# Loading each token's channels once instead of twice, with a new assignment of channels to partitions

## The chip, the cores and the metric

One core of a Trainium2 chip. The metric is the device time of one execution, in microseconds (us). Kernels that are compared ran on the same chip in the same group; each group has its own runs of the kernel before. The profile's span starts and ends inside the execution. In most executions it is 1.7 to 1.9 us shorter than the device time, in a few 2.2 to 2.4 us.

TensorE multiplies matrices, and its results go to banks of a memory called PSUM; VectorE, ScalarE and GpSimd compute element by element. The DMA engines move data: a transfer is issued from the queue of an engine, is cut into pieces, each a contiguous run of bytes, and lands later. Memory on the core has 128 partitions (rows).

## The reference

A causal convolution along the sequence (7 taps, softmax-normalised, one set of taps for each group of 24 channels), then a two-layer network with an exact GELU between its matrices.

```python
x = randn(8, 4096, 192) * 0.1        # batch, sequence, channels
weight = randn(8, 7) * 0.3           # heads, taps
w = softmax(weight, axis=-1)
conv[b, s, h, g] = sum_k w[h, k] * x_padded[b, s + k, h, g]   # 24 channels g a head
h = conv.reshape(32768, 192) @ w_in  # 192 x 2048
out = gelu_exact(h) @ w_out          # 2048 x 192, out is float32
```

## The kernel before

Tokens run in two halves. A block takes w tokens of each half (w is 256 for blocks 0 to 5, then 512, 35 blocks in all). The 128 partitions are four quadrants of 32: quadrant q holds half q//2 of the tokens, and one of two sets of channels, by q%2. Each of the three slices p of a block has 64 channels a token half: partition j of the half, slice p, is channel 64p+j. So quadrant q%2=0 needs channels 0-31, 64-95 and 128-159, and q%2=1 the others. The load doesn't pick them out: each quadrant loads the whole rows (less 32 floats) in one contiguous run per partition, and x comes in twice.

```python
def load(e, n, qs=(0, 2, 1, 3), sm=None):      # e: the engine that issues
    mb = WS[n] // 32
    if n >= NX:
        e.wait_ge(S_TR, NP * (n - NX + 1))
    for q in qs:
        off = ((q // 2) * HALF + OFF[n]) * D + 32 * (q % 2)
        e.dma_start(
            ap(xin[n % NX], 32 * q * (TB // 32 * D),
               [[TB // 32 * D, 32], [1, mb * D - 32]]),
            ap(xt, off, [[mb * D, 32], [1, mb * D - 32]]),
        ).then_inc(sm or S_XIN[n % NX], 16)
...
# VectorE, slice p of block n: 32x32 transposes, tokens by channels -> channels by tokens
v.transpose(
    ap(xT[n % 2], p * XW + HL, [[NP * XW, 128], [1, w]]),
    ap(xin[n % NX], 64 * p, [[TB // 32 * D, 128], [D, w // 32], [1, 32]]),
).then_inc(S_TR)
```

Around it: VectorE convolves on the transposed x (in blocks 0 and 1 TensorE does that, with diagonal matrices), TensorE multiplies by W_in, ScalarE applies GELU, TensorE multiplies by W_out, and VectorE transposes the result for the store. Engines work in order. The start on GpSimd, whose queue also carries the transfers that convert to bf16, is

```python
for i in range(3):
    win_in(FP[i], FP[i + 1], S_WIN[i])     # W_in, 6 transfers
g.wait_ge(S_IDN, 2)
halo(0)                                    # needs block 0's transposes
load(g, 1, SW[1], S_XG[1])                 # 2 transfers
load(g, 2, SW[2], S_XG[2])                 # 4 transfers
g.dma_start(... wout ... woutt ...).then_inc(S_WOUT, 16)
halo(1)
load(g, 3, SW[3], S_XG[3])                 # 4 transfers
```

## Time and profile before

| | before |
|---|---|
| median of 3 runs | 687.19 us (686.70 to 687.27) |
| profiled execution | 687.63 us, span 685.8 us |
| TensorE busy | 677.9 us (99%) |
| VectorE busy | 563.0 us (82%) |

The rows of the page that the change touches, first the input transposes (after the bar: busy time, mean ns of one), then the transfers of x and W_out (KB each, median us from issue to landing):

```profile
L476 DVE STREAM_TRANSPOSE xT<-xin 128x512 f32<-128x512 f32 (+1 forms) x105 | 61.4, 635 | 2.4 <-issue 2.0
...
xin<-in_x_dram SPq DMA_DIRECT2D x116, 380.0 KB, 6.8
...
xin<-in_x_dram POOLq DMA_DIRECT2D x10, 188.0 KB, 5.9
wout<-in_moe_w_out_dram POOLq DMA_DIRECT2D x1, 768.0 KB, 11.2
```

A reader should see that the 116 large x loads alone are 45 MB for an x of 25.2 MB, and that they land in 6.8 us (median) while a block of 512 takes 20.7 us.

### The profile page before, as it was taken

To read this page: it belongs to the slowest core of one execution; us is meant where nothing else is said; L and a number is where in the kernel's file an instruction comes from. 1 tells how busy PE (TensorE), PEld (TensorE's weight loads), DVE (VectorE), ACT (ScalarE), POOL (GpSimd) and SP (SyncE) were. 2 spreads that over 40 slices of the span, in tenths; PEclk is the share of its full clock that TensorE was granted. 3 is DMA by queue.
4 is the path that set the end of the run, shared out by engine and by line. 5 is a ranking of instruction groups with operands and counts; after the bars stand their busy time and mean duration, and the time that the engine had idled before them with its cause. 6 is when DMAs were issued, how large, how long until landed. Compare 5 with 4: busy or idle time off the path is not lost.

```text
span 685.8 us, 27314 instructions
## 1 busy us (share of the span) xinstructions
PE 677.9 (99%) x12548; PEld 409.1 (60%) x12548; DVE 563.0 (82%) x914; ACT 532.0 (78%) x536; POOL 45.3 (7%) x97
## 2 busy tenths in 40 slices
PE   8999999999999999999999999999999999999997
PEld 4799755555555555555555555555555555555556
DVE  6999978888898888898888898888898888988602
ACT  6788987777787877778777877777878777777771
POOL 7110000000000000000000000000000000000000
PEclk9999999999999999999999999999999999999999
DMA  9657851456543566434566434565344665431224
GB/s 200 131 142 168 201 125 24 118 139 140 114 91 91 125 139 140 105 86 98 132 139 139 96 87 99 138 140 134 90 89 108 139 140 123 93 86 27 48 49 94
DMA packets 74418, 78.25 MB, mean 114 GB/s; under 512 B 64576, under 2 KB 69824, under 8 KB 70592
## 3 DMA queue, kind: packets, MB, share of 16 engines
q1 hardware_dynamic: 69776, 72.24, 46.0%
q0 software_dynamic: 3792, 3.50, 2.9%
q8 instruction: 98, 1.61, 1.1%
q10 hardware_dynamic: 736, 0.78, 0.4%
q14 instruction: 16, 0.13, 0.1%
HBM read 52.90 MB, written 25.17 MB: 114 GB/s over the span
## 4 chain that ended last, share of the span: by engine, by line
PE 94%; DMA 2%; ACT 1%; POOL 1%; issue 0%; DVE 0%
PE hp L681 47%; PE ob L745 42%; PE ob L712 5%; DMA wout<-in_moe_w_out_dram 2%; ACT gT L610 1%; DMA xin<-in_x_dram 1%; POOL xin L256 0%; POOL xTb L366 0%; ACT osb L225 0%; ACT L556 0%; DVE osb L245 0%; DVE osb L227 0%; DVE xT L476 0%
## 5 line engine op out<-in xcount | busy, mean ns | idle before, releaser
L610 ACT ACTIVATE gT<-hp 128x1024 bf16<-128x1024 f32 x512 | 522.9, 1023 | 135.2 <-PE hp L681 132.0
L681 PE MATMUL hp<-xc,win 64*64 64x512 bf16 (+2 forms) x6048 | 418.5, 366 | 1.0 <-ACT gT L610 0.7
L745 PE MATMUL ob<-gT,wout 64*64 64x512 bf16 x5376 | 366.3, 376 | 0.0
L506 DVE SCALAR_TENSOR_TENSOR acc<-xT,wcol,acc 128x512 f32<-128x512 f32 (+1 forms) x495 | 314.1, 699 | 0.0
L681 PEld LDWEIGHTS hp<-xc,win 64*64 64x64 bf16 (+1 forms) x6048 | 187.7, 106 | 135.6 <-ACT gT L610 2.1
L745 PEld LDWEIGHTS ob<-gT,wout 64*64 64x64 bf16 x5376 | 172.1, 118 | 123.0
L245 DVE STREAM_TRANSPOSE osb<-ob 128x512 f32<-128x512 f32 x84 | 74.0, 883 | 104.4 <-PE ob L745 104.4
L506 DVE SCALAR_TENSOR_TENSOR xc<-xT,wcol,acc 128x512 bf16<-128x512 f32 (+1 forms) x99 | 65.1, 712 | 0.0
L476 DVE STREAM_TRANSPOSE xT<-xin 128x512 f32<-128x512 f32 (+1 forms) x105 | 61.4, 635 | 2.4 <-issue 2.0
L372 POOL COPY xT<-xT 128x558 f32<-128x558 f32 x33 | 21.5, 652 | 579.6 <-DVE xT L476 579.6
L499 DVE TENSOR_SCALAR acc<-xT,wcol 128x512 f32<-128x512 f32 (+1 forms) x99 | 56.2, 619 | 1.1
L712 PE MATMUL ob<-wout,gT 64*128 64x192 bf16 x1024 | 52.2, 243 | 1.7 <-DMA wout<-in_moe_w_out_dram 1.4
L712 PEld LDWEIGHTS ob<-wout,gT 64*128 64x128 bf16 x1024 | 43.6, 94 | 7.9 <-DMA wout<-in_moe_w_out_dram 1.7
L355 POOL COPY xT<-xT 128x18 f32<-128x18 f32 x30 | 11.6, 386 | 1.1 <-DVE xc L459 1.1
L227 DVE COPY osb<-ob 128x384 f32<-128x384 f32 x4 | 2.2, 558 | 7.8 <-PE ob L712 7.8
L623 PE MATMUL hp<-warm 128*128 128x512 bf16 x16 | 6.3, 577 | 1.3 <-DVE warm L392 1.3
L225 ACT ACTIVATE osb<-ob 128x384 f32<-128x384 f32 x12 | 5.8, 486 | 0.0
L638 PE MATMUL ob<-xTb,dg 64*64 64x256 bf16 x84 | 5.3, 271 | 0.5 <-DVE xTb L452 0.5
L638 PEld LDWEIGHTS ob<-xTb,dg 64*64 64x64 bf16 x84 | 4.3, 107 | 1.6 <-DVE xTb L452 0.8
L623 PEld LDWEIGHTS hp<-warm 128*128 128x128 bf16 x16 | 2.1, 136 | 5.0 <-issue 3.6
L256 POOL DMA_DIRECT2D xin<-in_x_dram x10 | 5.0, 509 | 0.0
L437 DVE COPY win<-win 64x768 bf16<-64x768 bf16 (+1 forms) x6 | 3.2, 526 | 0.9 <-DMA win<-in_moe_w_in_dram 0.8
(32 smaller groups left out, 21.5 us busy)
## 6 DMA issues: line engine op xcount, KB each, us to landing
xin<-in_x_dram SPq DMA_DIRECT2D x116, 380.0 KB, 6.8
out_dram<-osb SPq DMA_DIRECT2D x112, 192.0 KB, 3.6
out_dram<-osb SPq DMA_DIRECT2D x56, 48.0 KB, 2.6
xin<-in_x_dram SPq DMA_DIRECT2D x12, 188.0 KB, 3.6
xin<-in_x_dram POOLq DMA_DIRECT2D x10, 188.0 KB, 5.9
wout<-in_moe_w_out_dram POOLq DMA_DIRECT2D x1, 768.0 KB, 11.2
win<-in_moe_w_in_dram POOLq DMA_DIRECT2D x4, 96.0 KB, 4.2
win<-in_moe_w_in_dram POOLq DMA_DIRECT2D x2, 192.0 KB, 5.2
```

The costliest lines, as they stand in the source:

```text
L245: v.transpose(ap(osb[m % 2], j, [[8 * C, 128], [C // 2, TB // 32], [NP, 32]]), bank(ring(m, j)),).then_inc(S_EV)
L355: g.tensor_copy(dst, ap(xT[(n - 1) % 2], WS[n - 1] + 31, [[NP * XW, 128], [XW, NP], [32, HB]],),).then_inc(S_HALO)
L372: g.tensor_copy(ap(t, 1, [[NP * tw, 128], [tw, NP], [32, HB], [1, 31]]), ap(t, WS[n], [[NP * tw, 128], [tw, NP], [32, HB], [1, 31]]),).the ...
L476: v.transpose(ap(xT[n % 2], p * XW + HL, [[NP * XW, 128], [1, w]]), ap(xin[n % NX], 64 * p, [[TB // 32 * D, 128], [D, w // 32], [1, 32]],) ...
L499: ins = v.tensor_scalar(a, src, wk, None, ALU.mult)
L506: ins = v.scalar_tensor_tensor(dst, src, wk, a, op0=ALU.mult, op1=ALU.add)
L610: a.activation(out=ap(gT[n % 2], i * c * 2 * w, dst), in_=ap(hp[u % 2], 0, src), func=AF.Gelu,).then_inc(S_GELU)
L623: t.matmul(hp[1][:, 0:512], warm[:, 0:128], warm[:, :])
L638: ins = t.matmul(bank(CONVB[n][p], r, w), dg[r, d0 : d0 + 64], xTb[PC[n]][r, x0 : x0 + w], start=(k == KS - 1), stop=(k == 0), tile_positi ...
L681: ins = t.matmul(hp[u % 2][fo : fo + fw, o : o + w], win[r, f1 : f1 + fw], xc[n % 2][r, p * TB : p * TB + w], start=(p == 0), stop=(p == N ...
L712: ins = t.matmul(bank(bb[sub], w=C), gT[m % 2][r, c0 : c0 + 128], wout[r, CH[i] * C : (CH[i] + 1) * C], start=(ph == 0 and i == 0), stop=( ...
L745: ins = t.matmul(bank(ring(m, j), slice(64 * h, 64 * h + 64), w), ap(wout, 64 * hf * NF * C + CH[i] * C + j, [[NF * C, 64], [NP, 64]],), g ...
```

## The change

Its intent is to load x once. A quadrant loads a contiguous half of a token's channels, and channel 3c+p of it becomes slice p of partition c. A load's run is then 96 floats a token (384 B), the transposes read every third float, and the rows of W_in and the channels of the taps follow.

```diff
+    DQ = D // 2
-        xin = [sbt("xin%d" % i, [128, TB // 32 * D], F32) for i in range(NX)]
+        xin = [sbt("xin%d" % i, [128, TB // 32 * DQ], F32) for i in range(NX)]
# load
-                off = ((q // 2) * HALF + OFF[n]) * D + 32 * (q % 2)
+                off = ((q // 2) * HALF + OFF[n]) * D + DQ * (q % 2)
-                        32 * q * (TB // 32 * D),
-                        [[TB // 32 * D, 32], [1, mb * D - 32]],
+                        32 * q * (TB // 32 * DQ),
+                        [[TB // 32 * DQ, 32], [DQ, mb], [1, DQ]],
-                    ap(xt, off, [[mb * D, 32], [1, mb * D - 32]]),
+                    ap(xt, off, [[mb * D, 32], [D, mb], [1, DQ]]),
# W_in
-                        ap(wint, hf * FH + c0, [[F, 64], [64 * F, NP], [1, c1 - c0]]),
+                        ap(wint, hf * FH + c0, [[NP * F, 64], [F, NP], [1, c1 - c0]]),
# taps
-                    ap(wch, 32 * (q % 2), [[D, 32], [64, NP], [1, 32]]),
+                    ap(wch, DQ * (q % 2), [[D, 32], [1, NP], [NP, 32]]),
# input transposes
-                        64 * p,
-                        [[TB // 32 * D, 128], [D, w // 32], [1, 32]],
+                        p,
+                        [[TB // 32 * DQ, 128], [DQ, w // 32], [NP, 32]],
```

## The prediction

> **What bounds the kernel now.** I read the page's busy row first, then the chain of work that ended last, then the waits, then the order of instructions on VectorE and GpSimd in the first 100 us.
>
> ```profile
> span 685.8 us, 27314 instructions
> PE 677.9 (99%) x12548; PEld 409.1 (60%) x12548; DVE 563.0 (82%) x914; ACT 532.0 (78%) x536; POOL 45.3 (7%) x97
> ...
> DMA packets 74418, 78.25 MB, mean 114 GB/s; under 512 B 64576, under 2 KB 69824, under 8 KB 70592
> ...
> PE 94%; DMA 2%; ACT 1%; POOL 1%; issue 0%; DVE 0%
> ```
>
> TensorE is busy for all but 8 us, and 94% of the chain is its own matmuls. So a transfer that is halved can win only where TensorE stands still. The table by stretch tells where that is (columns: stretch, length, busy time of PE, PEld, DVE, ACT, POOL, clock, DMA share, GB/s).
>
> ```profile
> 20.00:25.00 5.00, 3.61 (x76) 3.10 (x72) 5.00 (x14) 2.96 (x3) 0.27 (x1) 1.00 0.52 121
> 25.00:74.00 49.00, 48.87 (x1040) 45.81 (x1036) 48.82 (x107) 40.38 (x46) 4.11 (x9) 1.00 0.65 154
> ...
> 91.00:655.00 564.00, 564.00 (x10458) 320.18 (x10460) 474.21 (x723) 446.09 (x437) 24.93 (x51) 1.00 0.48 109
> ```
>
> From 91 to 655 us TensorE has no gap at all; from 20 to 25 us it is idle for 1.4 us. VectorE is full from 25 to 74 us, which will matter below. The chain names what the gap waits for:
>
> ```profile
> 8.22 3.01 POOL xin L256 x6
> 11.23 11.22 DMA wout<-in_moe_w_out_dram
> 22.50 0.67 PE ob L712 x12
> ```
>
> The first output matmul needs W_out. GpSimd issues that transfer at 11.23, behind six x loads, and it lands 11.22 us later because the DMA engines are saturated (share 1.0 and more in each 2 us stretch from 4 to 22 us). The waits give the share of this that TensorE feels: 1.4 us once, and no other wait of TensorE above 0.7 us.
>
> ```profile
> PE ob L712 <- DMA wout<-in_moe_w_out_dram: 1.4, 1, 1.4
> DVE osb L245 <- PE ob L745: 104.4, 30, 11.8
> ```
>
> The second line is VectorE's slack: in the steady state it stands about 3 us in each 20.7 us block for TensorE.
>
> **What the Trainium skill says.** Three places bear on it.
> "DMA: Bandwidth & Descriptors", Specifications, puts the smallest transfer at line rate at 512 B. The new pieces of x are 96 floats = 384 B. The trace has pieces of that size already, the output stores: from 620 to 640 us only one block's stores run, with a DMA share of 0.19, so 0.19 x 20 us x 16 engines / 2048 packets = 30 ns of an engine for one packet, or 786 KB in 3.8 us = 207 GB/s. The loads' 12160 B rows: the steady share 0.48 x 20.7 us = 9.9 us a block, less 3.8 for the stores, leaves 6.1 us for 1.556 MB = 255 GB/s. So small pieces are slower per byte, as the page has it, but only by a fifth, for half the bytes.
> "Advanced Engine Details and Errata", SBUF Cachelines, says lines are 16 bytes and that an access pattern which changes the line at each access pays. A step of three floats is 12 bytes: of four reads only two share a line. No transpose in the trace reads with that step, but the output transpose writes with it: 883 ns against 681 for the input transpose at the same 512 columns.
> "VectorE: DVE Perf Modes", the section on the TRN2 errata, gives PSUM sources 120 cycles of fixed cost against 58, so up to 65 ns of those 202 can be PSUM; the rest, 137 to 202 ns, is the step, if reading costs what writing costs. I take 0.17 us at 512 columns and 0.085 at 256 as my estimate.
>
> **The change, part by part.**
> *Loads of x.* A 512-token block goes from 4 x 32 rows of 12160 B to 4 x 512 pieces of 384 B: 1.556 MB and about 6.1 us of DMA time become 786 KB and, at 30 ns a piece, 3.8 us. A 256-token block goes from 770 KB (about 3.0 us at the same 255 GB/s) to 1024 pieces, 1.9 us. In all, x read falls from 49.8 MB to 25.2 MB, while the packets rise by 480 for each of 116 large issues and 224 for each of 24 small ones, 61,056 in all, to about 135,500. After 26 us nothing waits for these transfers: they are issued three blocks ahead (over 40 us) and land in under 9. Gain there: 0.
> *The start.* Blocks 0 to 3 are loaded before W_out lands. Four times 1.1 us less DMA time puts its landing at about 22.4 - 4.4 = 18.0, plus what its issue is delayed. TensorE arrives at 21.1. So the whole 1.39 us of the wait goes: -1.4 us.
> *GpSimd's descriptors.* Its ten x loads go from 32 pieces to 256. Two other issues give the price: 192 pieces took 655 ns (W_in), 2048 took 1394 (W_out): 0.40 ns a piece. So 490 ns becomes about 580, six of them before W_out are +0.54 us, still far from the 3 us it would need to bring the wait back.
> *Block 1.* VectorE stands 1.96 us before the transposes of block 1 (12.11 to 14.07); GpSimd's halo copy that they need ended at 12.89, so the load came last, and it comes sooner now. The halo copy moves to about 12.89 + 0.54 + 0.3 (next point) = 13.7. So block 1 starts some 0.3 us sooner; TensorE, which waited 0.51 us for it at 15.45, gains about 0.2: -0.2 us.
> *Taps and the first transposes.* The four 96-column transposes of the taps read with the step: 4 x 0.03 = +0.13 us; the three of block 0: 3 x 0.085 = +0.26. The first was started at 6.37, 0.04 us after VectorE had finished its previous work, so an earlier load of block 0 wins nothing, and the added time moves the first convolution by some 0.3 us. Most of it is met again in the waits between ScalarE and TensorE in block 0; the 0.2 above has it counted in.
> *W_in.* Same pieces, same bytes, another row order: 0.
> *Transposes, steady state.* 87 x 0.17 + 18 x 0.085 = +16 us of VectorE, busy 563 to about 579. Per block 0.5 us, out of its wait of 3 us before the first output transpose of a block. That wait is for TensorE's second pass, so what comes after it, the last convolution taps, keeps its distance to TensorE: 0 us.
> *Transposes, 25 to 91 us.* Here VectorE has no waits and its work runs a little ahead. Its results for block 6 were ready at 71.64 and TensorE took them up at 74.93: margin 3.3. Block 7: 87.15 and 90.97, margin 3.8. TensorE now arrives 1.6 us sooner; VectorE starts block 2 about 0.3 sooner, then carries 3 x 0.085 for each of blocks 3, 4, 5 and 3 x 0.17 for 6 and 7: +1.0 net by block 6, +1.5 by block 7. Left: 0.7 us in both. No loss, but nearly none to spare.
> *Store and load issue on the sync queue.* The loads' issue grows from 0.43 us to what a store of as many pieces takes, 0.8; the queue waits for 414 us of the span: 0.
> Sum: -1.4 - 0.2 = -1.6 us, so 687.19 - 1.6 = 685.6.
>
> **The rivals.**
> *The step costs VectorE more.* If each strided read took two cycles, 512 columns would cost 681 + 533 = 1214 ns. By block 7 VectorE would be 0.8 x 4 + 1.6 x 2 - 0.5 = 5.9 us later against a margin of 3.8: TensorE would wait some 2 us more than before in all, and the gain at the start is swallowed by the same wait. In the steady state 1.6 us a block still fits into 3. Time: about 689.5. For it: the page on cachelines, and a full VectorE from 20 to 74 us. Against it: the write with the same step costs 0.2 us, not 0.53.
> *GpSimd's descriptors cost more.* At 1 us an issue instead of 0.58, the halo copy of block 1 comes at 16 and TensorE loses about 2 us there; W_out, then issued at 14.3, still lands before TensorE comes. Time: about 687.5. For it: ten issues with eight times the pieces, and VectorE's copies of W_in run beside them. Against: 2048 pieces in 1.39 us.
> *Nothing at all moves*, because the first 20 us are set by VectorE and ScalarE and W_out's landing is bound by something other than bytes (its own 2048 pieces of 768 B): 687.2. Against: the DMA share of over 1.0 at 182 to 277 GB/s with four queued x loads in it.
> *VectorE becomes the bound* all along: it would need over 1 us more per transpose. 700 us or more; nothing in the profile speaks for it.
>
> **Range and chances.** Predicted 685.6. Best case, a free step and more won in block 0 and 1: 684.3. Worst within eight in ten, the step at two cycles: 689.5. A change of 2% is 13.7 us; TensorE's idle time is 8 us in all, of which the change touches 2, so faster by over 2% cannot follow (1%). Slower needs VectorE to become the bound (2%). Within 2%: 97%.
>
> **What would show it.** HBM read falls from 52.9 to about 28.3 MB and packets rise to about 135,500; if not, I read the loads wrongly. The wait of TensorE for W_out is gone and the transfer lands near 19 us. The input transpose of 512 columns takes 0.82 to 0.88 us and VectorE's busy time is near 579; over 1.1 us brings a wait of TensorE for the convolution near 73 or 89 us and makes the prediction wrong upwards. The x issues on GpSimd take near 0.58 us. VectorE's wait for TensorE before output transposes falls from 104 to about 90 us.

## More of the kernel before

The sync queue and ScalarE's queue each issue two of block 0's four loads.

## The result, and the profile after

| | before, same chip | changed | ratio (95% interval) |
|---|---|---|---|
| first measurement | 686.95 us, 4 runs | 686.56 us, 4 runs | 0.9998 (0.9981 to 1.0015) |
| control, run later | 686.51 us, 11 runs | 686.52 us, 5 runs | 0.9997 (0.9986 to 1.0009) |

A ratio is the mean time of one kernel's fast runs over that of the other's fast runs of the same rounds, so it isn't quite the ratio of the medians in the table. Within 0.2% the change does nothing to the time.

Its page, in the lines that answer to those of before:

```profile
span 684.5 us, 27314 instructions
## 1 busy us (share of the span) xinstructions
PE 677.3 (99%) x12548; PEld 409.0 (60%) x12548; DVE 580.5 (85%) x914; ACT 532.6 (78%) x536; POOL 46.0 (7%) x97
...
DMA packets 133234, 53.66 MB, mean 78 GB/s; under 512 B 127552, under 2 KB 132960, under 8 KB 133120
...
HBM read 28.31 MB, written 25.17 MB: 78 GB/s over the span
...
L478 DVE STREAM_TRANSPOSE xT<-xin 128x512 f32<-128x512 f32 (+1 forms) x105 | 78.5, 799 | 0.2 <-DMA xin<-in_x_dram 0.2
...
xin<-in_x_dram SPq DMA_DIRECT2D x116, 192.0 KB, 4.4
...
xin<-in_x_dram POOLq DMA_DIRECT2D x10, 96.0 KB, 2.7
wout<-in_moe_w_out_dram POOLq DMA_DIRECT2D x1, 768.0 KB, 8.6
```

The bytes read fell from 52.9 to 28.3 MB, loads land in 4.4 us instead of 6.8, and VectorE carries 17.5 us more. TensorE's work is the same.

By stretch (columns as in the prediction):

```profile
20.00:25.00 5.00, 4.92 (x100) 4.14 (x96) 5.00 (x14) 3.99 (x4) 0.27 (x1) 1.00 0.34 84
25.00:74.00 49.00, 48.93 (x1040) 45.88 (x1038) 48.86 (x105) 40.47 (x46) 3.62 (x8) 1.00 0.46 99
...
91.00:655.00 564.00, 564.00 (x10460) 320.21 (x10456) 490.34 (x727) 446.19 (x436) 25.97 (x53) 1.00 0.35 75
```

The start, in single lines: first of the kernel before, then of the changed one (start, length, engine, line; in square brackets: idle time before, and what ended it):

```profile
14.07 1.10 DVE L476 STREAM_TRANSPOSE xT<-xin 128x256 f32<-128x256 f32 x3 [1.96 <-issue]
```
```profile
12.49 1.20 POOL L383 DMA_DIRECT2D wout<-in_moe_w_out_dram  x1
12.59 1.34 DVE L478 STREAM_TRANSPOSE xT<-xin 128x256 f32<-128x256 f32 x3
21.11 0.67 PE L714 MATMUL ob<-wout,gT 64*128 64x192 bf16 x12
```

Block 1's transposes no longer wait, W_out is issued later than before (11.23), and the first output matmul has no wait.

In this profile the gap of 1.4 us between 20 and 25 us is gone. If that were the change's doing, it should be 1.3 us faster, as the two spans are (685.8 and 684.5). The timed runs don't show it. That contradiction is what the experiments had to settle.

The chain of waits of the changed kernel no longer goes through GpSimd and W_out, but through block 0's load and the first convolution:

```profile
2.04 4.96 DMA xin<-in_x_dram
7.00 0.02 issue
7.03 0.53 DVE xT L478
7.55 0.02 issue
7.58 0.43 ACT xTb L572
8.00 0.04 issue
8.04 2.50 PE ob L640 x42
```

Block 0, with half the bytes, lands at 7.00 us. Before, it landed at 6.34 (the chain there has a DMA piece from 1.70 of 4.64 us). The first convolution starts at 8.04 instead of 7.48.

### The profile page after: what moved, and what is told of

It is laid out like the page before. It is cut to its first block, busy times and chain, and to the rows that moved or that the text cites. A ratio compares the mean times of both kernels' runs of the same rounds, so it can differ in the third digit from the quotient of the medians.

```text
span 684.5 us, 27314 instructions
## 1 busy us (share of the span) xinstructions
PE 677.3 (99%) x12548; PEld 409.0 (60%) x12548; DVE 580.5 (85%) x914; ACT 532.6 (78%) x536; POOL 46.0 (7%) x97
## 2 busy tenths in 40 slices
DMA packets 133234, 53.66 MB, mean 78 GB/s; under 512 B 127552, under 2 KB 132960, under 8 KB 133120
## 3 DMA queue, kind: packets, MB, share of 16 engines
q0 software_dynamic: 3792, 2.56, 2.4%
## 4 chain that ended last, share of the span: by engine, by line
PE 96%; ACT 2%; DMA 1%; issue 0%; DVE 0%; SPq 0%
PE hp L683 47%; PE ob L747 42%; PE ob L714 6%; ACT gT L612 2%; PE ob L640 1%; DMA xin<-in_x_dram 1%; ACT osb L227 0%; DVE osb L247 0%; SPq L258 0%; DVE osb L229 0%; DVE xT L478 0%; ACT xTb L572 0%; SPq L795 0%; ACT xc L579 0%
## 5 line engine op out<-in xcount | busy, mean ns | idle before, releaser
L247 DVE STREAM_TRANSPOSE osb<-ob 128x512 f32<-128x512 f32 x84 | 73.7, 880 | 86.8 <-PE ob L747 86.8
L478 DVE STREAM_TRANSPOSE xT<-xin 128x512 f32<-128x512 f32 (+1 forms) x105 | 78.5, 799 | 0.2 <-DMA xin<-in_x_dram 0.2
L357 POOL COPY xT<-xT 128x18 f32<-128x18 f32 x30 | 11.6, 387 | 1.4 <-DVE xc L461 1.4
L324 POOL DMA_DIRECT2D win<-in_moe_w_in_dram x6 | 3.9, 651 | 0.0
```

Source lines behind the costliest of these rows:

```text
L247: v.transpose(ap(osb[m % 2], j, [[8 * C, 128], [C // 2, TB // 32], [NP, 32]]), bank(ring(m, j)),).then_inc(S_EV)
L357: g.tensor_copy(dst, ap(xT[(n - 1) % 2], WS[n - 1] + 31, [[NP * XW, 128], [XW, NP], [32, HB]],),).then_inc(S_HALO)
L478: v.transpose(ap(xT[n % 2], p * XW + HL, [[NP * XW, 128], [1, w]]), ap(xin[n % NX], p, [[TB // 32 * DQ, 128], [DQ, w // 32], [NP, 32]],),) ...
```

## The experiments

Four theories stood against each other. (A) The prediction's: halved bytes end the wait for W_out, worth 1.4 us. (B) The wait belongs to the one profiled execution and neither kernel. (C) Pieces, not bytes, decide how fast loads are. (D) The slower transposes cost time.

### The changed kernel again, as control

No edit.

> The changed kernel once more, as the control of this group. If the first measurement holds, it is within 0.2% of the kernel before, 0.4 to 1.3 us shorter in the median, and its profile again has no wait of TensorE for W_out while the first convolution starts near 8.0 us instead of 7.5. If the difference is only noise, the sign changes and the start of the first convolution scatters in both kernels.

Measured: 686.52 us, ratio 0.9997 (0.9986 to 1.0009). TensorE again has no wait for W_out, and the first convolution starts at 8.54 us. The start of the changed kernel is thus late in both profiles, and the time is the same as before.

### W_out ahead of block 2's loads, in the kernel before

```diff
             load(g, 1, SW[1], S_XG[1])
-            load(g, 2, SW[2], S_XG[2])
             g.dma_start(... wout ...).then_inc(S_WOUT, 16)
+            load(g, 2, SW[2], S_XG[2])
```

> The kernel before with one edit: W_out is issued ahead of block 2's loads, so it no longer queues behind them; x is still loaded twice. Theory (the change gains only by ending the 1.4 us wait for W_out): the wait is gone, the first output matmul starts near 21.1 us and the span is about 684.5, as short as the changed kernel. Block 2's x then lands 2 to 3 us later, and VectorE, which runs ahead by 3.3 us at block 6, loses that much; so TensorE may wait up to 1 us near 73 us. Rival (the halved bytes help elsewhere too): the span stays at 685.5 or more.

Measured: 692.26 us, ratio 1.008 (1.0067 to 1.0093): slower by 0.8%, a loss that neither side named (the rival's "685.5 or more" takes it in only because it is open upwards). The wait for W_out is gone, but VectorE works in order, and its stream has the transposes of block 2 ahead of the last two convolution outputs of block 1. VectorE, then TensorE (in square brackets: idle time before, and what ended it):

```profile
15.95 0.42 DVE L459 CAST xc<-ob 128x256 bf16<-128x256 f32 x1 [0.51 <-PE ob L638]
21.51 1.10 DVE L476 STREAM_TRANSPOSE xT<-xin 128x256 f32<-128x256 f32 x3 [5.14 <-DMA xin<-in_x_dram]
22.54 0.39 DVE L459 CAST xc<-ob 128x256 bf16<-128x256 f32 x1
```
```profile
19.13 0.83 PE L681 MATMUL hp<-xc,win 64*128 64x256 bf16 x12
23.07 0.60 PE L681 MATMUL hp<-xc,win 64*128 64x256 bf16 x4 [3.11 <-DVE xc L459]
```

VectorE stood 5.14 us for block 2's load, and TensorE 3.11 us for an output that had nothing to do with block 2. What the order of issue gives W_out it takes from block 2, which had no margin: in the first profile of the kernel before VectorE already stood 0.44 us for it. The stand is not the whole loss. After it TensorE's granted clock was 0.50 from 24 to 26 us (0.78 in the 2 us before, 0.87 in the 2 us after), and the 12 first output matmuls took 1.17 us instead of 0.67. All six runs have a mean clock of 0.995 to 0.998, the kernel before 0.999 or 1.000. W_out itself, with only two loads ahead of it in its queue instead of six, still took 9.5 us to land, though block 2's loads now followed right behind it. That speaks against the prediction's sum, which takes the saved time of all the loads before it off its landing.

### Loads of 128 B pieces in the old layout

```diff
-                        [[TB // 32 * D, 32], [1, mb * D - 32]],
+                        [[TB // 32 * (D // 2), 32], [D // 2, mb], [32, NP], [1, 32]],
-                    ap(xt, off, [[mb * D, 32], [1, mb * D - 32]]),
+                    ap(xt, off, [[mb * D, 32], [D, mb], [64, NP], [1, 32]]),
# transposes: offset 32 * p, rows of D // 2; W_in and taps untouched
```

> The kernel before with only the loads changed: each quadrant loads its own channels of the old layout, three pieces of 32 floats (128 B) a token, so x is loaded once; transposes, taps and W_in as before, no read with a step. If bytes decide (rival), W_out lands sooner, the 1.4 us wait goes, and without the slower transposes the span is 684 to 684.5. If the number of pieces decides (theory): 6144 packets a block of 512 at 20 to 30 ns are 8 to 11.5 us of DMA time a block, more than the 9.9 for loads and stores of before together; block 0 lands 2 to 4 us later, W_out later than in the kernel before, and the span is 688 to 692; after 90 us nothing waits for the loads still.

Measured: 687.97 us, ratio 1.0019 (1.0007 to 1.0031), between the two expectations. Block 0 lands at 7.35 us, 1.0 later than in the first profile of the kernel before (2 to 4 were expected), the first convolution is late (8.31 us), and W_out is issued at 13.44 instead of 11.23. So (C) fits the first load and the issues, in this one profile. It doesn't fit W_out's own transfer, which took 8.7 us, as in the changed kernel; and the 0.83 us for which TensorE waits for it lie within the scatter shown further down. Nor does it hold for the DMA engines' time. Over 300 us of the steady state, for the kernel before, the changed one and this one:

```profile
300.00:600.00 300.00, 300.00 (x5568) 170.32 (x5564) 256.60 (x392) 236.70 (x233) 13.79 (x28) 1.00 0.51 116
```
```profile
300.00:600.00 300.00, 300.00 (x5566) 170.34 (x5560) 263.19 (x391) 236.94 (x232) 13.81 (x28) 1.00 0.37 80
```
```profile
300.00:600.00 300.00, 300.00 (x5568) 170.30 (x5560) 256.20 (x392) 236.91 (x232) 13.79 (x28) 1.00 0.44 79
```

TensorE is busy for all of the 300 us in all three. The DMA share is 0.51, 0.37 and 0.44, times 20.72 us a block: 10.6, 7.7 and 9.1 us; less 3.8 for the stores, a block's loads take 6.8, 3.9 and 5.3 us. By this estimate a piece of 128 B is 5.3 x 16 / 6144 = 14 ns, not the 20 to 30 that I expected.

### The new layout with the old, whole-row loads

```diff
 # changed kernel, but
-                        [[TB // 32 * DQ, 32], [DQ, mb], [1, DQ]],
-                    ap(xt, off, [[mb * D, 32], [D, mb], [1, DQ]]),
+                        [[TB // 32 * D, 32], [1, mb * D - DQ]],
+                    ap(xt, off, [[mb * D, 32], [1, mb * D - DQ]]),
```

> The changed kernel with the loads of before: the new channel layout (transposes reading every third float, taps and W_in with it), but whole rows loaded twice. Theory: VectorE's transposes cost 0.86 us as in the changed kernel and its busy time is near 580, yet nothing is gained since the bytes are not halved: the wait of 1.4 us for W_out is back, the first convolution starts near 7.7 us (no late landing of block 0, only the slower tap transposes), and the span is 685.8 to 686.2, the same as before within noise, since VectorE's extra 0.5 us a block lies in its wait. Rival (strided transposes cost time): the span is 687.5 or more.

Measured: 686.87 us, ratio 0.9999 (0.9987 to 1.0011). The first half of the theory holds: VectorE is busy for 579.6 us and the time is as before, so (D) falls. The other half fails: with the bytes doubled again, TensorE didn't wait for W_out at all; it landed in 9.1 us. What lies between this run and the changed kernel is the halving of bytes, and it bought nothing that the times show. (A) was in trouble, and the kernel before had to be profiled again.

### The kernel before, profiled three more times

No edit.

> The kernel before, unchanged, profiled again. Its first profile came from an execution of 687.6 us, 1.1 above the median of its eleven later runs, and the run with the old loads in the new layout showed no wait for W_out. If the 1.4 us wait of TensorE for W_out belongs to the kernel (the prediction's view), it is here again, W_out taking 11 us to land, span 685.5 to 686. If it belongs to single executions (rival), W_out lands in 9 to 10 us, the wait is under 0.7 us and the span is near 684.7.

> As for the first repeat of the kernel before: the same two theories with the same numbers; three profiles of one kernel show how far W_out's landing and the wait for it scatter.

> As for the first repeat of the kernel before: the wait for W_out is 1.4 us each time (prediction's view), or it scatters between 0 and 1.4 us from one execution to the next (rival).

Measured: the wait is 0.60, 0.46 and 0.21 us, the spans 684.6, 684.9 and 685.1 us. This line of the third repeat is the one that read 22.50 us and 1.39 in the profile on which the prediction rests:

```profile
21.80 0.67 PE L712 MATMUL ob<-wout,gT 64*128 64x192 bf16 x12 [0.21 <-DMA wout<-in_moe_w_out_dram]
```

(B) holds for the size of the wait: it is never as long again in these three, and the first profile caught the longest of the four. It does not hold for the wait as such, which is there each time. The repeats ran on chip 4 and the first profile's chip is not on record; but the waits of 1.24 and 1.67 us in the table below are of chip 4 too, so the chip doesn't explain the 1.39.

All profiles together. The two kernels with extra VectorE work, told below, start as the kernel that they come from, for the extra work comes after 70 us:

| profile | first convolution | from it to block 1's | W_out lands after | TensorE waits for it | first output matmul | span | span less that |
|---|---|---|---|---|---|---|---|
| before, first | 7.48 | 7.97 | 11.2 | 1.39 | 22.50 | 685.8 | 663.3 |
| before, repeats | 7.50, 7.38, 7.45 | 7.54, 8.01, 8.48 | 9.7, 10.1, 10.6 | 0.60, 0.46, 0.21 | 21.30, 21.51, 21.80 | 684.6, 684.9, 685.1 | 663.3, 663.4, 663.3 |
| before, VectorE work added at block 7 | 7.74 | 7.41 | 9.6 | 0.47 | 21.27 | 684.7 | 663.4 |
| before, VectorE work added from block 9 | 7.46 | 7.58 | 10.4 | 1.24 | 21.94 | (686.2) | - |
| before, W_out first | 7.41 | 7.55 | 9.5 | none | 24.95 | 689.1 | 664.2 |
| changed | 8.04, 8.54 | 7.40, 7.40 | 8.6, 8.4 | none | 21.11, 21.43 | 684.5, 684.9 | 663.4, 663.5 |
| changed, VectorE work added at block 7 | 7.76 | 7.40 | 10.2 | 1.67 | 22.49 | 685.8 | 663.3 |
| changed, VectorE work added from block 9 | 7.83 | 7.40 | 8.6 | none | 20.92 | (698.3) | - |
| new layout, whole rows | 7.70 | 7.63 | 9.1 | none | 20.83 | 684.5 | 663.7 |
| 128 B pieces | 8.31 | 7.41 | 8.7 | 0.83 | 22.20 | 685.6 | 663.4 |
| changed, block 0 as whole rows | 7.47 | 7.40 | 8.4 | none | 20.36 | 683.9 | 663.5 |

Three things are to be seen. The last column is nearly constant: from the first output matmul on, the kernels differ by 0.4 us at most (W_out first, with its lower clock, aside), so the start decides the time of all these kernels. The wait for W_out scatters in both: the six starts of the kernel before, all but the run with W_out first, average 0.73 us of it; the changed kernel's four have none three times and 1.67 us once, 0.42 on average. And TensorE comes from the first convolution to block 1's in 7.40 or 7.41 us in all six starts that load x once from block 1 on, but in 7.41 to 8.48 in the eight that load it twice, for there VectorE, and TensorE after it, waits for block 1's data.

With these columns the change can be added up (means of six starts before and of four changed): the first convolution comes 0.54 us later (7.50 to 8.04), the way to block 1's is 0.43 us shorter (7.83 to 7.40), and the wait for W_out is 0.31 us shorter. That is -0.20 us, and the first output matmul comes at 21.72 us before and at 21.49 in the changed kernel: 0.2 us, as little as the ratios say. So the halved bytes did win something at the start, and the late first convolution took it away. The starts are few, and the third term hangs on a single wait of 1.67 us; the second shows in five of the six starts of before.

### Block 0 alone as whole rows, in the changed kernel

```diff
 # load, n == 0 only: own buffer xblk, whole rows twice
+                if n == 0:
+                    e.dma_start(
+                        ap(xblk, 32 * q * (mb * D), [[mb * D, 32], [1, mb * D - DQ]]),
+                        ap(xt, off, [[mb * D, 32], [1, mb * D - DQ]]),
+                    ).then_inc(sm or S_XIN[n % NX], 16)
+                    continue
 # trans, n == 0: reads xblk, offset p, [[w // 32 * D, 128], [D, w // 32], [NP, 32]]
```

> The changed kernel, but block 0 alone is loaded as whole rows (twice, as before) into a buffer of its own; blocks 1 and up as in the changed kernel. Theory: the late start of the changed kernel (block 0 lands at 7.0 to 7.5 us instead of 6.3, and ScalarE issues its two loads in 1.34 us instead of 0.89, which holds up the exponential of the taps by 0.27 us) comes from generating 256 pieces a transfer. Then block 0 lands by 6.4, the first convolution starts near 7.7 instead of 8.0 to 8.5, and the span is 0.3 to 0.8 us shorter, 684.0 to 684.3, provided that W_out lands by 20.7. Rival (the late start is scatter): no difference in the first convolution's start beyond 0.2 us.

Measured: 685.67 us, against 686.74 for the kernel before in the same group (the changed kernel wasn't in it), ratio 0.9987 (0.9973 to 1.0001). The first convolution starts at 7.47 us, earlier than in any of the changed kernel's four starts (7.76 to 8.54), and ScalarE's issue of its two loads is back from 1.34 to 0.89 us, the exponential of the taps from 2.69 to 2.42 us. Block 0's data is there by 6.45 us, when VectorE takes it up without a wait; in two of the changed kernel's four starts it came at 7.00 and 7.50 (in the other two VectorE took it up at 6.75 and 6.81, also without a wait). Twice the bytes came no later here, and sooner than in two of the four. The issue doesn't grow in proportion to the pieces, though: ScalarE's two loads took 1.39 us with 768 pieces each (the 128 B run), hardly more than the 1.34 with 256. The chain of waits of this run no longer has block 0's load in it; it runs through the taps on VectorE:

```profile
5.29 1.16 DVE dg L435 x2
6.45 0.53 DVE xT L485
7.00 0.43 ACT xTb L581
7.47 2.50 PE ob L649 x42
```

The gains of the halved bytes stay: block 1's convolution follows after 7.40 us, there is no wait for W_out, and the first output matmul at 20.36 us is the earliest of all profiles. This is what the sum above asks for. The kernel is 1.1 us faster than the one before in the medians, and its five spans are 683.8 to 684.6 us against 683.9 to 685.5; but the interval of the ratio just reaches 1, and the gain is far from 2%.

### Four memsets ahead of block 7, in both kernels

VectorE's lead at blocks 6 and 7 was read off as in the prediction: 0.67 and 0.70 us in the changed kernel's first profile, 0.61 and 0.63 in the second, 2.5 and 3.1 in the first repeat of the kernel before.

```diff
+                if b == 7:
+                    for k_ in range(4):
+                        v.memset(spare[k_][:, :], 0.0).then_inc(S_SPARE)
```

> The changed kernel with four more VectorE instructions, memsets of 128x512 into spare buffers, once, ahead of block 7: by the trace's 272 ns for half that size about 0.55 us each, 2.2 us together. Theory: the slower transposes have used up VectorE's lead at block 7 (0.7 us left in two profiles), so TensorE waits 1.5 us for block 7's convolution near 90 us, and the time from the first output matmul to the end is 1.5 us longer than the 663.4 us of all runs so far. Rival (VectorE's lead is regained elsewhere and does not matter): no wait.

> The same four memsets ahead of block 7 in the kernel before, whose lead at block 7 was 3.1 to 3.8 us. Theory: 2.2 us fit into the lead, TensorE does not wait, and the time from the first output matmul to the end stays 663.3 to 663.5 us. Rival (any added VectorE work delays the end): 1.5 us longer here as well.

Measured: the kernel before with the memsets takes 686.52 us, ratio 0.9998 (0.9985 to 1.0012), with no wait at block 7, as the theory has it. The changed kernel with them takes 687.55 us, ratio 1.0013 (0.9997 to 1.0028). The time points the way that the theory says, but the profile can't confirm it. In this execution W_out came late, TensorE stood 1.67 us for it, and so it also came late to block 7:

```profile
22.49 0.67 PE L723 MATMUL ob<-wout,gT 64*128 64x192 bf16 x12 [1.67 <-DMA wout<-in_moe_w_out_dram]
```

Block 7's convolution was ready at 90.69 us and TensorE took it up at 90.97. So my expectation of a wait of 1.5 us failed. Whether 2.1 us of added work cost time in the executions with a prompt W_out stays open. The times can't tell: with W_out prompt TensorE would have come to block 7 1.67 us sooner, at 89.30, and stood until 90.69, so that the execution would have been only 0.28 us shorter (an estimate from this trace), and the four spans are 685.8 to 686.0 us. What the run does show is that the changed kernel has the wait for W_out too.

### Six memsets ahead of every block from 9 on, in both kernels

```diff
+                if b >= 9:
+                    for k_ in range(6): ...   # as above
```

> The changed kernel with six such memsets (about 3.3 us) ahead of every block from 9 to the last: more than VectorE's wait of 2.46 us a block. Theory: VectorE sets the pace, each of some 25 blocks is 0.8 us longer, about +20 us (range 10 to 30, for the memset's duration is an estimate). Rival (the wait on VectorE is only put off, not used up, since TensorE waits elsewhere): under +5 us.

> The same six memsets a block in the kernel before, where VectorE waits 3.0 us a block. Theory: each block is about 0.54 us less long than in the changed kernel with the same memsets, the price of the three slower transposes; over 25 blocks some 13 us less, so about +7 us (0 to 17) against the kernel before. Rival: no difference between the two kernels under this load.

Measured: 700.6 us, ratio 1.0205 (1.0189 to 1.022) in the changed kernel, and 688.42 us, ratio 1.0026 (1.0012 to 1.0041) in the one before. Six memsets take 3.2 us. Both theories' numbers fall inside the ranges that I gave. The changed kernel's VectorE now sets the pace, and TensorE waits for it:

```profile
PEld ob L756 <- DVE osb L250: 17.0, 19, 1.0
PE ob L756 <- DVE osb L250: 7.9, 19, 0.5
```

These are its waits between 200 and 600 us. It isn't the convolution that comes late, as I had thought, but the output transposes: TensorE's next pass needs the PSUM bank that they empty. From one group of memsets to the next it is 21.34 us in the changed kernel (mean of 19 blocks, from 193.24 to 598.76 us) and 20.83 in the other (192.26 to 588.09), whose TensorE needs 20.72. The difference, 0.51 us, is about the price of three slower transposes (3 x 0.18 = 0.54). It costs nothing today and 12 us in a kernel with 3 us more VectorE work a block.

## Why the prediction was right or wrong

The range and the chances held: 684.3 to 689.5 and 97% for no change beyond 2%, measured 686.56. The centre, 685.6, was 1 us too low, and the gain of 1.6 us that it named was not found: the ratios are 0.9998 and 0.9997, uncertain by about 1 us. That the centre came this near is partly luck. It was counted from 687.19, the median of three runs; one more run made that 686.95, and the later groups gave 686.51 and 686.74. And the range was wide enough to hold no gain at all. Step by step:

- *TensorE is the bound, loads after 26 us are hidden.* Right. Between 300 and 600 us TensorE has no gap in either kernel, and the kernel with whole rows in the new layout takes the same time with twice the bytes.
- *The loads' size.* Right: 28.3 MB are read, and a block's loads take 3.9 us of the DMA engines (predicted 3.8). The saving was larger than predicted: the 6.1 us of before were read from 91 to 655 us, which takes in the stretch after the last load (issued at 599 us); from 300 to 600 us they are 6.8. So the smaller pieces are slower per byte by about a tenth (202 against 229 GB/s), not by a fifth. The packets came to 133,234, not 135,500: the ten loads that GpSimd issues count as many packets as before (the row of that queue stays at 3,792), and 10 x 224 = 2,240 is what I had too many.
- *"So the whole 1.39 us of the wait goes: -1.4 us."* This is the step that failed, and in two ways. The 1.39 us were those of one execution: over six starts of the kernel before the wait averages 0.73 us and goes down to 0.21, and in the changed kernel it averages 0.42, so 0.31 us of it went. And the landing was wrongly sized. I had 18.0 us plus what the issue is delayed. In the changed kernel's first profile W_out is issued at 12.49 us and lands 8.6 us later, at 21.1, just as TensorE arrives. It took 8.84 us on average (five starts of the kernels without doubled rows past block 0, in 384 B pieces) against 10.27 before (six starts): 1.4 us less, not 4.4. The issue meanwhile came 1.0 us later, at 11.9 to 13.0 us in those profiles against 11.1 to 11.6. Most of the gain on the transfer was given back in its issue. Why the landing scatters from one execution to the next (9.6 to 11.2 us before, 8.4 to 10.2 in the changed kernel) stays open.
- *GpSimd's descriptors.* Right: 588 ns an issue, predicted about 580. W_out's issue came 1.26 us later in the changed kernel's first profile: 0.84 because the loads ahead of it started later, behind block 0's halo, and 0.42 from the six longer issues (3.49 us instead of 3.07).
- *"an earlier load of block 0 wins nothing, and the added time moves the first convolution by some 0.3 us."* The load was later in two of four starts and in none seen to be earlier, and the first convolution moved from 7.50 us (mean of six starts) to 8.04 (mean of four), 0.5 us. The steps that were counted are right: the taps' four transposes took 1.28 us instead of 1.17, block 0's three 1.32 instead of 1.10. Left out was the issue. ScalarE's two loads took 0.45 us longer to issue, so the exponential of the taps started about 0.3 us later in all four starts. I had reckoned with the bytes of this load and not with the making of its pieces. Loading block 0 as whole rows undoes it: 7.47 us, in the one profile of that run.
- *Block 1: -0.2 us.* Right in the cause, and too small: the wait for its data went, 0.43 us on average. But the late start took it away: TensorE took up block 1's convolution at 15.16 to 15.94 us in the changed kernel, against 15.04 to 15.93 before. One reading was wrong: the transposes don't need the halo copy (tokens at a block's edge, for the convolution) that ended at 12.89 us, for in the changed kernel they start at 12.59 and that copy at 13.66.
- *The transposes.* Right: 862 ns at 512 columns (predicted 0.82 to 0.88 us), VectorE busy for 580.5 us (579), its wait before output transposes 86.8 us in all (about 90), and no time lost by it. The rival with two cycles a read (1214 ns) fell, and so did those of 1 us for a GpSimd issue and of VectorE as the bound. The rival by which nothing moves, 687.2, came nearer to the time (686.56) than the prediction did, but not for its reason: W_out's transfer did get shorter.
- *A lead of 0.7 us left at blocks 6 and 7.* Right as a reading (0.67 and 0.70). The experiment that was to show what it is worth was inconclusive.

## What to carry to other kernels

Before a wait of 1 us in a profile is counted as a gain, compare that execution with the timed runs, and profile the kernel again: here the one profile had a span of 685.8 us where the repeats had 684.6 to 685.1, and half of the wait was that execution's. Compare spans: the second repeat took 687.19 us by its device time and had a span of only 684.9. Halving a transfer's bytes by cutting it into more pieces can bring the first data later, so at the start, where nothing hides a load, try few long pieces even if bytes are read twice (here one kernel, about 1 us, with an interval that just reaches no gain). Moving work to an engine that has slack is free only until that slack is needed: measure what is left, as with the added memsets.

## What the Trainium skill lacked or had wrong

- "DMA: Bandwidth & Descriptors", Specifications, gives 512 B as the least transfer for line rate. The figure alone reads like a threshold; here the fall below it is gradual: from 300 to 600 us x came at 1556 KB / 6.8 us = 229 GB/s in runs of 12 KB, 786 KB / 3.9 us = 202 GB/s in 384 B and 786 KB / 5.3 us = 148 GB/s in 128 B (estimates from the DMA shares above).
- The same page, in its anatomy of one GpSimd-issued DMA, has descriptor generation as "small, variable" and fits one transfer as 2.0 us plus bytes at 436 GB/s. Here an issue's cost grew with the pieces, but less than in proportion: on GpSimd it was 490 and 585 ns (medians) for 32 and 256 of them. On the sync queue it was 430 ns (median) for 32 runs, 814 for 512 pieces and 1042 for 1536, and on ScalarE's two loads took 0.89 us with 32 runs each, 1.34 with 256 and 1.39 with 768; for those queues I found no figure by the number of pieces. W_out's 1.57 MB would be 5.6 us by the fit (an estimate from that page); beside the loads of x it took 8.4 to 11.2 us, and no run had it alone.
- "Advanced Engine Details and Errata", SBUF Cachelines, gives a penalty for changing 16-byte lines without a size. A VectorE transpose that reads fp32 with a step of 12 bytes took 862 ns against 681 at 512 columns, and 498 against 413 at 256; it is the step and not the load, for on whole rows it took 857 and without the step on 128 B pieces 677.
